# Threshold attention and a squared-ReLU layer on one core: where the second weight chunk's load stands among the loads of the second attention period

## Chip, cores and metric

The kernel runs on one core of a Trainium2 chip. Its time is device microseconds (us) of that core. A number given for a kernel is the median of three runs; a profile is one further execution, with its own time.

## The reference, cut to what matters

Attention over 8 batches of 8 heads, 576 positions, head size 64. A weight survives only where its score is within `tau` of the row's maximum. The result, reshaped to 4608 tokens of 512, goes through two matrices with a squared ReLU between them.

```python
scores = q @ k.T / 8
scores = where(scores >= max(scores) - tau, scores, -1e9)
attn = exp(scores - max(scores)); attn /= sum(attn) + 1e-9
x = (attn @ v).transpose(0, 2, 1, 3).reshape(4608, 512)
h = maximum(x @ w_in, 0)                 # w_in 512 x 2048
out = h * h @ w_out                      # w_out 2048 x 512
```

The two weight matrices arrive in eight-byte floating point: NumPy makes them so by the factor they are scaled with. q, k and v are four-byte.

## The kernel before

**Three stages.** First attention (to about 512 us of the profile), then the hidden layer, then the output layer. The two layers multiply 128x128 blocks by a scheme that saves products and pays with sums on VectorE (DVE) and GpSimd (POOL). The weights for them are brought in and made four bytes wide during attention, in 32 chunks.

**Attention in periods.** The heads are taken in 32 pairs (two heads side by side in 128 partitions). A pair's queries are cut into units of 128 rows; `period(p)` (L619) works on two units, A = 2p and B = 2p+1, and runs over p = -2 ... 74. Within one period:

- `SA`, `SB`: the scores of A and B on TensorE (PE), L434.
- `topA0` ... `topB1`: DVE copies the scores out of PSUM and takes each row's extreme, L452. `powA0` ...: the exponential on ScalarE (ACT), L462. `maskA0` ...: DVE masks and sums, L467. `least` and `over` are tiny POOL steps (L459, L474), `inv` is DVE's reciprocal (L477), which needs `over`.
- `U`, `V`, `W`: PE turns the masked weights of the periods before (L380, and L515 for the reciprocals, which needs `inv`); `eU`, `eV`, `eW` are ACT's copies of these out of PSUM (L523).
- `PV`: the product with the values (L532); `x` copies it out (L657 on ACT in a period that converts), `xm` scales it on POOL (L669) and queues it to be written out (L578).
- `T`: PE turns the queries or the keys of a pair that will be needed later (L398); `eT` has ACT copy them out (L403, L411) **and then asks for loads of a later pair** through `ask_ahead` (queries `load_q`, L294; keys `load_k`, L308, L315, L316).
- `fetch`: issues the load of one weight chunk, 512 KB, on SyncE's (SP's) DMA queue (L191). `c1` ... `c6` make a chunk four bytes wide: c1 on ACT (L205), c3 on POOL (L219), c2 on POOL (L212), and one period later c4 and c5 on DVE (L227, L235) and c6 on POOL (L245).

**What sets the order.** Every engine carries out its own instructions in the order in which the program issues them, and that order is a list of step names written by hand: `PLAIN`, `CONVERTING`, and in `BEGIN_WITH` (L602) lists of their own for periods 0 and 1. Nearly all loads and stores of this stage stand in one queue, SP's, in program order.

**Chunks and periods.** `fetch(begun(p + 2))` in period p loads the chunk whose c1 stands in period p + 2: chunk 0 is fetched in period 0, chunk 1 in period 1, chunk 2 in period 2. Period 2 is the first with the list `CONVERTING`, in which `fetch` is the first step and c1 stands ahead of `powA0`. A chunk lands in one of four buffers of its own, so the fetches of chunks 0 to 3 wait for no earlier user.

**Turns and loads.** `TURNS` puts the queries of pair 1 in period 0, its keys in period 1, the queries of pair 2 in period 2, its keys in period 3, the queries of pair 3 in period 4, its keys in period 5. `ask_ahead` of period 0 asks for the queries of pairs 2 and 3 (four loads), that of period 1 for the keys of pairs 2 and 3 (seven loads each), that of period 2 for the queries of pair 4.

So SP's queue holds, from period 0 on: chunk 0, four query loads, fourteen key loads, chunk 1, chunk 2, two query loads, and so on.

Of the kernel before, what the change touches and what calls it, by code (L numbers as in the profile page):

```python
# [48 lines left out]
def kernel(  # L49
# [539 lines left out]
    def begun(n):  # L589
# [15 lines left out]
            maskA0 maskA1 maskB0 maskB1  # L605
        """.split(),
        1: """
            SA SB T eT fetch over topA0 topA1 leastA inv V topB0 topB1 leastB powA0 powA1 eV W
            powB0 eW maskA0 maskA1 powB1 maskB0 maskB1
        """.split(),  # L610
    }
# [627 lines left out]
```

## Time and profile before

| what | value |
|---|---|
| median of three runs | 1308.43 us (1307.17 to 1308.57) |
| the profiled execution: time | 1308.95 us |
| the profiled execution: span, first to last instruction | 1307.2 us |
| mean granted TensorE clock | 0.995 |
| busy: PE, DVE, POOL, ACT | 98%, 77%, 70%, 65% of the span |
| chunk loads of `w_in` (512 KB each) | 16, median 4.5 us from issue to landing |
| loads of keys (64 KB) | 126, median 3.1 us from issue to landing |

The times of the profile are microseconds from the span's start. A row of the timeline gives start, duration, engine, line, operation, output and input, and in brackets how long the engine stood idle before and what released it. "SPq" rows are SP's issues of DMAs, not the transfers. Periods begin, by the first score product of `SA`, near 22 (SB of period 2 stands at 22.1), 27.9 (period 3), 38.0 (period 4) and 46.1 us (period 5).

### The profile page before, as it was taken

How to read it: one execution, taken by the hardware profiler on the slowest of the kernel's cores; microseconds unless marked ns; L12 is line 12 of the kernel's file. 1: busy time of each engine (PE TensorE's matmuls, PEld its weight loads, DVE VectorE, ACT ScalarE, POOL GpSimd, SP SyncE). 2: the span in 40 equal slices, each digit the busy share in tenths (PEclk: the TensorE clock that was granted, in tenths of full speed). 3: DMA queues.
4: the chain of work that ended last, by engine and by line, in shares of the span. 5: the costliest groups of instructions: out<-in, count | busy, mean ns of one | idle time of the engine just before them, and what ended most of it. 6: DMA issues, size and time to landing. Idle time of an engine off the chain costs nothing.

```text
span 1307.2 us, 47836 instructions
## 1 busy us (share of the span) xinstructions
PE 1283.6 (98%) x19463; PEld 1158.4 (89%) x19463; DVE 1010.1 (77%) x2431; ACT 846.1 (65%) x1498; POOL 915.6 (70%) x1023
## 2 busy tenths in 40 slices
PE   8899999999999999999999999999999999999998
PEld 5677777777777778999999999999999999999998
DVE  6899999999999996877787778777646654665463
ACT  5999999988999985657665766675523432433240
POOL 2778788765555320978897889768777777777775
PEclk8999999999999999999999999999999999999999
DMA  5665666544433313466656665579645224522511
GB/s 126 165 158 144 169 180 191 147 103 101 94 78 79 81 39 80 140 192 218 195 169 194 215 196 166 176 262 396 226 157 162 72 95 159 161 65 99 161 33 33
DMA packets 247035, 192.12 MB, mean 147 GB/s; under 512 B 97184, under 2 KB 195488, under 8 KB 246816
## 3 DMA queue, kind: packets, MB, share of 16 engines
q1 hardware_dynamic: 245504, 188.66, 48.0%
q8 instruction: 153, 2.51, 0.8%
q14 instruction: 66, 0.54, 0.1%
q10 hardware_dynamic: 1312, 0.41, 0.1%
HBM read 116.65 MB, written 72.35 MB: 145 GB/s over the span
## 4 chain that ended last, share of the span: by engine, by line
PE 88%; ACT 4%; DVE 3%; DMA 2%; issue 1%; SPq 1%; POOL 0%; ACTq 0%; POOLq 0%; DVEq 0%
PE ph L840 29%; PE po L975 29%; PE sc L532 10%; PE sc L434 10%; PE pt L380 5%; DVE arena L452 2%; PE sc L515 2%; PE sc L398 2%; ACT arena L462 2%; ACT arena L523 1%; PE sc L380 1%; DMA wall<-w 1%; DMA arena<-in_q_dram 1%; DMA g<-arena 0%; DMA arena<-in_moe_w_in_dram 0%
## 5 line engine op out<-in xcount | busy, mean ns | idle before, releaser
L125 POOL TENSOR_TENSOR arena<-arena 128x512 f32<-128x512 f32 (+1 forms) x314 | 377.8, 1222 | 134.9 <-DVE arena L125 116.6
L975 PE MATMUL po<-wall,arena 128*128 128x128 f32 x3528 | 395.0, 276 | 1.8 <-ACT arena L752 1.4
L975 PEld LDWEIGHTS po<-wall,arena 128*128 128x128 f32 x3528 | 394.3, 192 | 2.4 <-ACT arena L752 1.8
L840 PE MATMUL ph<-arena,wall 128*128 128x128 f32 x3528 | 394.2, 275 | 0.7 <-DVE arena L659 0.7
L840 PEld LDWEIGHTS ph<-arena,wall 128*128 128x128 f32 x3528 | 394.0, 192 | 0.8 <-issue 0.8
L125 DVE TENSOR_TENSOR arena<-ph,arena 128x512 f32<-128x512 f32 x378 | 256.4, 689 | 86.2 <-PE ph L840 66.3
L122 POOL TENSOR_TENSOR arena<-arena 128x128 f32<-128x128 f32 (+2 forms) x314 | 254.8, 812 | 48.8 <-DMA arena<-w 32.6
L467 DVE SCALAR_TENSOR_TENSOR arena<-arena 128x576 f32<-128x576 f32 x288 | 236.5, 857 | 2.2 <-ACT arena L462 1.3
L125 DVE TENSOR_TENSOR arena<-po,arena 128x128 f32<-128x128 f32 x378 | 108.3, 290 | 167.9 <-PE po L975 163.7
L452 DVE TENSOR_SCALAR_CACHE_REDUCE arena<-sc 128x576 f32<-128x576 f32 x288 | 205.2, 748 | 12.3 <-ACT arena L523 4.1
L462 ACT ACTIVATE arena<-arena 128x576 f32<-128x576 f32 x288 | 208.8, 774 | 8.1 <-DVE arena L452 5.1
L786 ACT COPY c<-arena 128x512 f32<-128x512 f32 (+1 forms) x303 | 173.5, 580 | 50.5 <-DVE arena L122 41.3
L532 PEld LDWEIGHTS sc<-arena 64*64 64x64 f32 x5760 | 159.2, 133 | 36.3 <-DVE arena L452 20.3
L532 PE MATMUL sc<-arena 64*64 64x128 f32 (+1 forms) x5760 | 180.4, 263 | 2.7 <-DVE arena L452 1.1
L434 PE MATMUL sc<-arena 64*64 64x64 f32 (+1 forms) x2304 | 177.5, 417 | 4.8 <-ACT arena L403 2.3
L122 DVE TENSOR_TENSOR arena<-arena,c 128x512 f32<-128x512 f32 (+1 forms) x267 | 174.9, 663 | 6.0 <-ACT c L786 4.0
L523 ACT COPY arena<-pt 128x1024 f32<-128x1024 f32 x144 | 146.2, 1016 | 29.7 <-PE pt L380 28.4
L752 ACT COPY arena<-po 128x128 f32<-128x128 f32 x63 | 16.6, 263 | 186.5 <-PE po L975 183.7
L380 PEld LDWEIGHTS pt<-ident,arena 64*128 64x128 f32 x2304 | 84.0, 140 | 40.9 <-ACT arena L523 28.3
L752 ACT COPY arena<-ph 128x512 f32<-128x512 f32 x63 | 36.6, 581 | 124.2 <-PE ph L840 123.7
L434 PEld LDWEIGHTS sc<-arena 64*64 64x64 f32 x2304 | 74.4, 134 | 42.7 <-issue 15.5
L380 PE MATMUL pt<-ident,arena 64*128 64x64 f32 x2304 | 102.8, 230 | 3.2 <-ACT arena L523 2.2
(51 smaller groups left out, 917.6 us busy)
## 6 DMA issues: line engine op xcount, KB each, us to landing
g<-arena SPq DMA_DIRECT2D x144, 256.0 KB, 2.5
arena<-g SPq DMA_DIRECT2D x144, 256.0 KB, 4.5
w<-arena SPq DMA_DIRECT2D x60, 256.0 KB, 2.4
wall<-w SPq DMA_DIRECT2D x49, 256.0 KB, 5.2
arena<-w SPq DMA_DIRECT2D x44, 256.0 KB, 3.0
arena<-in_v_dram SPq DMA_DIRECT2D x32, 288.0 KB, 3.9
out_dram<-arena SPq DMA_DIRECT2D x70, 128.0 KB, 2.2
arena<-in_q_dram SPq DMA_DIRECT2D x64, 128.0 KB, 3.8
```

What stands on the lines that cost most here:

```text
L122: e.tensor_tensor(out=out, in0=x, in1=y, op=ALU.subtract)
L125: e.tensor_tensor(out=out, in0=x, in1=y, op=ALU.add)
L380: made = nc.tensor.transpose(pt[:, r, ts(slot, HALF)], of[rows, :], ident[rows, rows])
L434: made = nc.tensor.matmul(sc[at, ds(to, count)], lhs, kT[rows, ds(at_k, count)], start=True, stop=True)
L452: made = nc.vector.tensor_scalar(out=s[:, j, :], in0=sc[:, ds(at, S)], scalar1=1.0, scalar2=None, op0=ALU.mult, op1=ALU.min, accum_out=nmx ...
L462: nc.scalar.activation(out=w[:, :, j, :], in_=of(j), func=AF.Exp, bias=nmx[:, j : j + 1], scale=-1.0)
L467: nc.vector.scalar_tensor_tensor(out=w[:, :, j, :], in0=of(j), scalar=thr[:, j : j + 1], in1=w[:, :, j, :], op0=ALU.is_le, op1=ALU.mult, a ...
L523: touch("weights", nc.scalar.copy(joined(to), whole(pt, 0, count)), at, 2 * BANK, m)
L532: made = nc.tensor.matmul(sc[ds(u * D, D), ds(5 * j * BANK + row, count)], loaded_v[i][rows, (c - (u != j)) % CH, :], wT[m][rows, ds(weigh ...
L786: nc.scalar.copy(c, y)
L840: nc.tensor.matmul(to[:, j, :], W_IN[m, k][:, ts(j, P)], of[k][:, m - 1, :], start=(not more and j == 0), stop=True, skip_group_check=True,)
L975: nc.tensor.matmul(to, g[:, j, :], w[:, j, :], start=(not more and j == 0), stop=(j == 3), skip_group_check=True)
```

## The change

In the list of period 1, `fetch` moves from behind `T eT` to the front. Nothing is added or removed: the same instructions are issued, and on SP's queue the load of chunk 1 (one DMA, L191) moves ahead of the fourteen loads of the keys of pairs 2 and 3 that `eT` of this period asks for.

```diff
         1: """
-            SA SB T eT fetch over topA0 topA1 leastA inv V topB0 topB1 leastB powA0 powA1 eV W
+            fetch SA SB T eT over topA0 topA1 leastA inv V topB0 topB1 leastB powA0 powA1 eV W
             powB0 eW maskA0 maskA1 powB1 maskB0 maskB1
         """.split(),
```

## The prediction

> **What bounds the kernel now.** I read from the whole to the place of the change. The page gives PE 98% of the span and 88% of the chain that ended last, but that is a mean over three stages. A table by stretches of 25 us (columns: span of the stretch, then busy us and instructions of PE, PE's weight loads, DVE, ACT, POOL, then clock, DMA share, GB/s) shows what is full in the attention stage:
>
> ```profile
> 43.00:68.00 25.00, 24.91 (x656) 19.48 (x657) 25.00 (x68) 24.07 (x47) 19.77 (x26) 1.00 0.55 143
> ...
> 218.00:243.00 25.00, 24.61 (x581) 18.11 (x582) 25.00 (x70) 24.33 (x43) 20.66 (x27) 1.00 0.70 194
> ```
>
> DVE is busy for 25.00 of 25.00 us in these two, and for at least 24.94 in each of the eight stretches from 43 to 243 us. From 43 us on, whatever brings DVE to a given instruction earlier moves all that follows; before 43 us DVE has holes. Next, who waits for the chunk that the change moves. The waits of ACT between 28 and 43 us:
>
> ```profile
> ACT arena L205 <- DMA arena<-in_moe_w_in_dram: 3.3, 1, 3.3
> ```
>
> One wait of 3.3 us, for a weight chunk, at L205, which is c1. The chain that ended last passes through it (start, duration, what):
>
> ```profile
> 28.96 0.60 SPq L316
> 29.56 0.04 issue
> 29.60 4.73 DMA arena<-in_moe_w_in_dram
> 34.33 0.02 issue
> 34.35 0.02 ACT arena L205
> ```
>
> So chunk 1 is issued at 29.60, right behind the last of the key loads, lands at 34.33, and ACT stands from 31.02 to 34.35. What this does to DVE (timeline of DVE, rows with idle time, and the one before):
>
> ```profile
> 33.03 0.42 DVE L227 TENSOR_SCALAR arena<-arena 128x512 int32<-128x512 int32 x1
> 36.32 0.18 DVE L477 RECIPROCAL arena<-arena 128x4 f32<-128x4 f32 x1 [2.86 <-POOL arena L474]
> ...
> 41.14 0.76 DVE L452 TENSOR_SCALAR_CACHE_REDUCE arena<-sc 128x576 f32<-128x576 f32 x1 [0.57 <-PE sc L398]
> ...
> 42.99 0.76 DVE L452 TENSOR_SCALAR_CACHE_REDUCE arena<-sc 128x576 f32<-128x576 f32 x1 [0.41 <-issue]
> ```
>
> The first hole is the chunk's: c1 on ACT, then c3 and `over` on POOL (L474 at 36.05), then `inv`. The other two are its echo: PE waited 2.22 us for `inv` and 1.00 us for ACT's `x`, and then ran period 4 at half clock:
>
> ```profile
> 35.78:39.19 3.41, 1.64 (x36) 1.24 (x38) 2.87 (x8) 3.41 (x9) 3.17 (x4) 1.00 0.93 269
> 39.19:42.60 3.41, 3.41 (x48) 1.91 (x38) 2.76 (x7) 2.82 (x5) 2.67 (x4) 0.50 0.18 39
> ```
>
> PE was busy 1.64 of 3.41 us, and in the next 3.41 us the granted clock was 0.50; L434's eight products (SB) took 1.84 us there against 1.09 in period 3. [...]
>
> **What the change removes and adds.** No instruction is added. On SP one issue moves past the fourteen key loads that `eT` of period 1 asks for. SP's timeline from there:
>
> ```profile
> 14.27 2.03 SPq L294 DMA_DIRECT2D arena<-in_q_dram  x4
> 16.34 4.42 SPq L308 DMA_DIRECT2D arena<-in_k_dram  x2
> ...
> 24.30 0.60 SPq L316 DMA_DIRECT2D arena<-in_q_dram  x1
> ```
>
> *The fetch itself.* It would be issued at 16.34. SP holds the first key load there for 3.76 us (to 20.1), an issue that elsewhere takes 0.6; the profile names no semaphore for it, and 4 query loads, chunk 0 and values are under way. I take it that the fetch is held likewise: issue over by 20.1 at the latest. Landings in the trace follow the order of issue: chunk 0 20.29, the four query loads 20.84, 21.45, 22.16, 22.64. Chunks issued back to back land 1.56 us apart (34.33, 35.89), so chunk 1 lands near 22.64 + 1.56 = 24.2; with the 4.73 us of its own row from 20.1, 24.8. ACT asks for it at 31.02: **6 us of slack**, the wait of 3.33 us is gone.
>
> *The keys of pair 2*, seven loads, are what the fetch now stands ahead of. Before, they are issued to 24.91 and the last lands at 27.07; T of period 3 turns them at 29.80, so there are 2.7 us of slack. The fetch costs SP one issue, 0.43 to 0.5 us, and its 1.56 us of transfer lie in the queue while SP needs 0.6 us for each key load anyway, so most of that is hidden. I take the last landing at 27.6 (one issue later); the upper end is 28.7 (0.5 + 1.56 - 0.4). Both are before 29.80. The keys of pair 3 come half a us later and are wanted in period 5, at 48.
>
> *The rest of SP's queue.* As many issues stand ahead of chunk 2 as before, so it is still issued near 30, but without chunk 1 ahead of it lands near 34.5 and not at 35.89.
>
> **Period 3 again, without the wait.** ACT: c1 at 31.02, the exponentials 31.6 to 33.7, `eT` to 34.5, `x` to 34.9 (PV is over at 34.06). POOL's `over` came 1.97 us after c1's start (36.32 - 34.35), so at 33.0; DVE ends L227 at 33.45, so `inv` follows with no hole: 2.86 us won. Behind it DVE has its five instructions of period 3 (36.32 to 40.57, 4.25 us) and ends at 37.7. PE: W's last part at 34.3 instead of 36.55, SA of period 4 at 34.9 instead of 38.01; PE has no gap left worth a clock spell, so at full clock T is over at 37.4 (1.4 + 0.7 + 0.5) and SB at 38.5. DVE's first copy of period 4 needs T: 37.4 against 37.7, the 0.57 is gone. Its third needs SB: 38.5 against 39.1, the 0.41 is gone. **What is late next**: chunk 2 at 34.5 against ACT's c1 near 38.1, and POOL, which works on to 39.2 and then does c3 with `over` at 40.4 against DVE's `inv` at 40.9. Both hold, the last by 0.5 us only.
>
> Sum: 2.86 + 0.57 + 0.41 = **3.84 us**, all of them holes of the engine that has none for the next 200 us. After that, order and dependences are the same and start earlier; the only transfer on the chain up to 500 us is a store of 2.22 us at 263.68, itself started by POOL's work. In the layers PE is full and starts earlier. Against the profiled execution: 1308.95 - 3.84 = 1305.1. That execution is 0.5 us above the median of the runs, so the median becomes 1308.43 - 3.84 = **1304.6 us**.
>
> Where I chose: if the clock spell is only luck and comes all the same, 2.86 us are won (1305.6). If a full 3.33 us of ACT plus the difference of the two periods' lengths (38.01 to 46.12 is 8.11, the next 6.76: 1.35) were won, it would be 4.7 us (1303.7), but DVE has not that many holes. Half-clock spells around 18.7 to 25.5 us may shift from run to run as well; by the same 1.35 us I bound that to either side.
>
> **Rivals.**
>
> 1. *The keys take the chunk's place.* SP stays blocked at the first key load until chunk 1 is through, at 24.2: then the other six are issued as before (24.91 - 20.11 = 4.8 us) to 29.0, and the last lands 2.16 us later, at 31.2. T of period 3 is 1.4 us late, DVE's first copy with it: 3.84 - 1.4 = 2.4 won, 1306.0. For it: the 3.76 us hold happened in just this place. Against it: two chunks back to back were issued in 1.68 us and two query loads behind them in 0.93, with no such hold.
> 2. *Slower.* The same place, but held twice: the fetch leaves SP only at 20.5, the first key load waits until it has landed (20.5 + 4.73 = 25.2), seven issues at their pace end at 30.6 and land at 32.8, and the 0.9 us by which one L315 was late before (1.49 against 0.6) comes on top: 33.7. T is 3.9 us late, which eats the gain; PE's gap brings the half clock back (0.98 of DVE holes). 3.84 - 3.9 - 0.98 = 1.0 lost: 1309.4. It decides from a landing at 32.7 on, which is 5.6 us later than before.
> 3. *The chunk shares the engines with the queries in front of it.* Queries of pair 2 land at 21.45 and PE waits for them (0.44 us, then DVE 1.68). If chunk 1's packets take turns with theirs, T of period 2 is up to 1.56 us later: 2.3 won, 1306.1. Against: the landings were in order of issue. [...]
> 4. *Given back later*: the chain is elastic somewhere behind 243 us, where DVE has holes again (24.2 of 25), and nothing is left: 1308.4.
>
> **Chances.** The forecast 0.71 (its own range 1303.4 to 1305.8), rivals 1 and 3 together 0.14, rival 4 0.06, rival 2 (slower) 0.09. The range takes in the forecast's and rivals 1 and 3 with the spread of the runs: 1303.0 to 1307.4. A measurement here tells about 0.2% (2.6 us) from no change: faster by more than that takes the forecast and a share of rivals 1 and 3, 0.74; within it 0.17; slower 0.09.
>
> **What would show it.** Right: ACT's L205 of period 3 starts near 31.0 with no wait for the chunk; `inv` directly behind L227 at 33.5; SA of period 4 near 34.9; clock 1.00 around 36 to 40; DVE at its first copy of period 5 near 44.9 instead of 48.70, and full from 30 us on. Rival 1 or 2: L398 of period 3 waits for a key load. Rival 3: L398 of period 2 starts later than 21.49. The forecast is wrong if chunk 1 lands after 31, or if DVE shows a new hole between 33 and 43 us, first of all before `inv` of period 4.

## The result, and the profile after

The changed kernel takes 1304.73 us (median of eight runs, 1302.06 to 1306.6), the kernel before 1308.53 us in the same series (median of eight, 1307.17 to 1310.59): 3.8 us less, a ratio of 0.9967 [0.9957, 0.9978] (in brackets, here and below, the 95% interval). Its profiled execution took 1305.30 us with a span of 1303.5; that of before 1308.95 with 1307.2. PE, DVE, ACT and POOL run the same instructions in the same order; only SP's queue differs.

**ACT.** The view of waits of ACT between 28 and 43 us is empty. Before, it held the wait of 3.3 us for the chunk and one of 0.6 us for PE at L523 (40.77), which the prediction left out. The timeline of ACT at period 3 shows c1 right behind the copy before it:

```profile
29.55 1.01 ACT L523 COPY arena<-pt 128x1024 f32<-128x1024 f32 x1
30.46 0.68 ACT L205 ACTIVATE arena<-arena 128x512 f32<-128x512 f32 x1
```

**DVE.** Its timeline of the changed kernel has no row with idle time between 30 and 45 us. The first copy of period 3, and the three places where there were holes:

```profile
30.13 0.75 DVE L452 TENSOR_SCALAR_CACHE_REDUCE arena<-sc 128x576 f32<-128x576 f32 x1
...
32.85 0.42 DVE L227 TENSOR_SCALAR arena<-arena 128x512 int32<-128x512 int32 x1
33.18 0.16 DVE L477 RECIPROCAL arena<-arena 128x4 f32<-128x4 f32 x1
...
37.20 0.75 DVE L452 TENSOR_SCALAR_CACHE_REDUCE arena<-sc 128x576 f32<-128x576 f32 x1
...
38.56 0.74 DVE L452 TENSOR_SCALAR_CACHE_REDUCE arena<-sc 128x576 f32<-128x576 f32 x1
...
44.27 0.74 DVE L452 TENSOR_SCALAR_CACHE_REDUCE arena<-sc 128x576 f32<-128x576 f32 x1
```

The last row is the first copy of period 5. The same two copies, of periods 3 and 5, in the kernel before:

```profile
30.32 0.75 DVE L452 TENSOR_SCALAR_CACHE_REDUCE arena<-sc 128x576 f32<-128x576 f32 x1
...
48.70 0.75 DVE L452 TENSOR_SCALAR_CACHE_REDUCE arena<-sc 128x576 f32<-128x576 f32 x1
```

From here on a **stretch** means the time from DVE's first copy (`topA0`) of period 3 to that of period 5: 18.38 us before, 14.14 after, so 4.24 us came out of these two periods.

**PE.** The table by windows, for the same 6.8 us as in the prediction (busy and instructions of PE, weight loads, DVE, ACT, POOL; clock; DMA share; GB/s):

```profile
35.78:39.19 3.41, 3.27 (x69) 2.09 (x68) 3.41 (x10) 3.38 (x6) 2.50 (x3) 1.00 0.63 177
39.19:42.60 3.41, 3.41 (x106) 2.87 (x98) 3.41 (x11) 3.30 (x8) 3.17 (x5) 1.00 0.30 58
```

The clock is 1.00 in both, and in the second of them PE gets 106 products done where it did 48.

**SP.** Its timeline shows the price of the move (start, duration of the whole group, line, what, how many):

```profile
17.37 2.55 SPq L191 DMA_DIRECT2D arena<-in_moe_w_in_dram  x1
19.96 1.26 SPq L308 DMA_DIRECT2D arena<-in_k_dram  x2
...
23.87 1.22 SPq L316 DMA_DIRECT2D arena<-in_q_dram  x1
```

The fetch is held for 2.55 us in the place where the first key load was held for 3.76; the key loads behind it go out at 0.6 us each, but for the last (L316), which takes 1.22. By the trace's landing records chunk 1 lands at 23.98, the last key load of pair 2 at 27.21, chunk 2 at 34.23.

**The chain that ended last** no longer holds a load between 16 and 44 us. Where it stood on the chunk's landing at 34.33 before and passed on through ACT, it now runs through PE's products and DVE's copies of period 4 (start, duration, what):

```profile
36.28 0.25 PE sc L398 x7
36.53 0.74 PE sc L434 x5
37.28 0.48 DVE arena L452
```

### The profile page after: what moved, and what is told of

The parts are those of the page before. It is cut to its first block, busy times and chain, and to the rows that moved or that the text cites. A ratio compares the mean times of both kernels' runs of the same rounds, so it can differ in the third digit from the quotient of the medians.

```text
span 1303.5 us, 47836 instructions
## 1 busy us (share of the span) xinstructions
PE 1283.4 (98%) x19463; PEld 1158.6 (89%) x19463; DVE 1010.0 (77%) x2431; ACT 846.2 (65%) x1498; POOL 914.6 (70%) x1023
## 4 chain that ended last, share of the span: by engine, by line
PE 87%; ACT 4%; DMA 3%; DVE 3%; issue 1%; POOL 1%; SPq 0%; ACTq 0%; POOLq 0%; DVEq 0%
PE ph L840 28%; PE po L975 28%; PE sc L532 11%; PE sc L434 10%; PE pt L380 5%; DVE arena L452 2%; DMA wall<-w 2%; PE sc L515 2%; PE sc L398 2%; ACT arena L462 1%; ACT arena L523 1%; PE sc L380 1%; DMA arena<-g 0%; DVE arena L125 0%; DMA g<-arena 0%
## 5 line engine op out<-in xcount | busy, mean ns | idle before, releaser
L523 ACT COPY arena<-pt 128x1024 f32<-128x1024 f32 x144 | 146.4, 1017 | 30.3 <-PE pt L380 29.1
```

Source lines behind the costliest of these rows:

```text
L523: touch("weights", nc.scalar.copy(joined(to), whole(pt, 0, count)), at, 2 * BANK, m)
```

## The experiments

A ratio is against the kernel before, run beside it (its medians were 1308.46 to 1309.2 us). Single runs of one kernel lie up to 4 us from its median, so the medians of kernels that differ by 1 us are not told apart. The stretch on DVE, taken from one profile each, is finer: behind the first copy of period 5 the rest of the span is 1258.4 to 1259.9 us in every kernel.

| kernel | ACT's wait for chunk 1 | stretch | half clock between 35 and 45 us | median, ratio |
|---|---|---|---|---|
| before | 3.33 | 18.38 | 39.19, for 3.41 us | 1308.53 |
| before, again (b1) | 4.54 | 20.38 | 36.47, for 6.83 | |
| before, again (b2) | 4.21 | 19.92 | 37.14, for 6.83 | |
| changed | none | 14.14 | none | 1304.73, 0.9967 |
| changed, again (a1) | none | 14.15 | none | 1303.98, 0.9964 |
| e1 | none | 14.13 | none | 1305.55, 0.9986 |
| e2 | 0.4 | 14.12 | none | 1305.98, 0.9982 |
| e3 | none | 14.13 | none | 1305.98, 0.9977 |
| e4 | none | 14.13 | none | 1304.3, 0.9974 |
| e5 | none (c1 late) | 15.44 | none | 1306.64, 0.9987 |
| e6 | 0.57 (c1 late) | 15.44 | none | 1305.37, 0.998 |
| g1 | none | 14.15 | none | 1304.22, 0.9968 |
| w1 | 2.02 | 22.07 | 37.86, for 6.83 | 1315.97, 1.0057 |
| w2 | 5.59 | 20.21 | 39.04, for 3.41 | 1308.5, 1.0003 |

The theory: ACT's wait for chunk 1 opened the hole ahead of `inv`, the other two holes followed from it, and any place of the fetch that lands the chunk before ACT asks for it gives the same gain. The rivals: the place itself matters, because the key loads, the query loads or SP pay for it; or the time came from something else that the new order brings, and not from the wait.

### e1: behind the keys of pair 2

```diff
-            asked[which] += 1
+            asked[which] += 1; fetch(1 if (which, asked[which]) == (1, 3) else None)
...
-            SA SB T eT fetch over topA0 topA1 leastA inv V topB0 topB1 leastB powA0 powA1 eV W
+            SA SB T eT over topA0 topA1 leastA inv V topB0 topB1 leastB powA0 powA1 eV W
```

> Chunk 1's fetch behind the seven key loads of pair 2 and ahead of those of pair 3. The theory (the whole difference is ACT's wait for chunk 1 ahead of the exponentials, and the DVE holes it makes): issued near 25, it lands near 29.7, still before ACT asks near 30.5 to 31; no wait, so the time of the changed kernel: 3.8 us below the kernel before, about 1304.7. Rival A (what counts is how early the chunk stands in the queue, since the order of the loads around it changes too): about half of the gain, 1306.6. Rival B (the clock spells decide, the load does not): the difference to the kernel before goes with the clock, not with the place.

Measured: 1305.55 us (twelve runs, 1304.54 to 1308.89), 0.9986 [0.9975, 0.9997]. The chunk was issued at 22.54 and landed at 27.70, with no wait of ACT and a stretch of 14.13. The keys of pair 2 had nothing new in front of them, and the stretch is that of the changed kernel, where the chunk stands ahead of them: there it took nothing from these keys that PE or DVE felt in the stretch. The median is another matter: by the ratio e1 wins 0.1% and the changed kernel 0.3%, and the two intervals barely overlap. Seven of e1's runs had a mean granted clock of 0.997 and took 1305.29 to 1306.71 us; the changed kernel's three runs with that clock took 1305.30 to 1306.60. But e1 has two runs at 0.996 (1308.70 and 1308.89) and none at 0.999 or 1.000, where the changed kernel has three (1302.06 to 1304.94). So the medians differ with the granted clock of the runs; whether the place of the load has a part in that is not shown.

### e2: among the keys of pair 3

```diff
-            queue = nc.scalar if i == 0 and j == 0 else nc.sync
+            fetch(1 if (i, j) == (3, 1) else None); queue = nc.scalar if i == 0 and j == 0 else nc.sync
...
-            SA SB T eT fetch over topA0 topA1 leastA inv V topB0 topB1 leastB powA0 powA1 eV W
+            SA SB T eT over topA0 topA1 leastA inv V topB0 topB1 leastB powA0 powA1 eV W
```

> Chunk 1's fetch amid the keys of pair 3, four loads ahead of its old place. The theory: issued near 27.2, landed near 31.9, ACT waits about 1.2 us; POOL's sum has 0.8 us to spare before DVE's reciprocal wants it, so a DVE hole of 0.3 to 0.6 us, no PE gap and no half clock in period 4: 3.2 to 3.5 us below before, about 1305.2. Rival A (one us of ACT's wait costs one us and more, as 3.33 us cost 4.25 us of DVE time between the first copies of periods 3 and 5): 1.2 us of wait cost 1.5 us, so 2.3 us below before, 1306.2.

Measured: 1305.98 us (twelve, 1303.63 to 1308.6), 0.9982 [0.9971, 0.9992]. The chunk landed at 29.75, earlier than expected, since SP's hold at the first key load was 1.78 us here and not 3.76. The view of ACT's waits:

```profile
ACT arena L205 <- DMA arena<-in_moe_w_in_dram: 0.4, 1, 0.4
```

That wait cost nothing: DVE had no hole and the stretch is 14.12. `inv` comes behind four copies and L227 on DVE, and a c1 that is 0.4 us late is still in time for it. So the price of a wait on ACT isn't its length, but what of it shows as a hole on DVE.

### e3: ahead of the queries of pair 2

```diff
         0: """
-            SA SB fetch topA0 T topA1 leastA topB0 topB1 leastB powA0 powA1 eT powB0 powB1
+            SA SB fetch fetch1 topA0 T topA1 leastA topB0 topB1 leastB powA0 powA1 eT powB0 powB1
...
+            "fetch1": lambda: fetch(1),
```

with the step taken out of the list of period 1.

> Chunk 1's fetch in period 0, right behind chunk 0 and ahead of the four query loads. The theory (landings in order of issue, 1.56 us for a chunk): the queries of pair 2 land near 22.9 instead of 21.3, and T of period 2, which stood at 22.3 in the changed kernel and waited for nothing, starts 0.6 to 1.5 us later; so 0.6 to 1.5 us slower than the changed kernel, about 1305.8, still 2.3 to 3.2 us below before. Rival (the transfers share the engines, so the place ahead of the queries costs them nothing more than the place behind): the time of the changed kernel, 1304.7.

Measured: 1305.98 us (twelve, 1303.77 to 1308.6), 0.9977 [0.9966, 0.9988], stretch 14.13. Here something pays in the profile, one period earlier. PE and DVE in period 2 of e3:

```profile
22.79 0.47 PE L398 MATMUL sc<-ident,arena 64*128 64x64 f32 x8 [1.29 <-DMA arena<-in_q_dram]
```

```profile
23.26 0.76 DVE L452 TENSOR_SCALAR_CACHE_REDUCE arena<-sc 128x576 f32<-128x576 f32 x1 [2.64 <-PE sc L398]
```

and DVE's same row in the changed kernel:

```profile
22.97 0.76 DVE L452 TENSOR_SCALAR_CACHE_REDUCE arena<-sc 128x576 f32<-128x576 f32 x1 [1.45 <-PE sc L398]
```

PE waits 1.29 us for queries that it did not wait for, and DVE's hole is 1.19 us larger. The transfers landed in the order of issue (queries of pair 2 at 22.10 and 22.65, behind the chunk at 21.69), which is what the prediction's third rival supposed of the other place and did not get there. But this hole is 0 to 1.7 us in the other thirteen profiles, so its size is not settled by one of e3. Nor did the loss reach period 3, which begins at 29.89 here and at 30.13 in the changed kernel's profile, whose early spell of half clock was longer (6.83 us against 3.41). The median can't show a loss of this size.

### e4: three chunks ahead of all the keys

```diff
-            SA SB T eT fetch over topA0 topA1 leastA inv V topB0 topB1 leastB powA0 powA1 eV W
+            fetch fetch2 fetch3 SA SB T eT over topA0 topA1 leastA inv V topB0 topB1 leastB powA0 powA1 eV W
...
+            "fetch": lambda: p in (2, 3) or fetch(begun(p + 2)), "fetch2": lambda: fetch(2), "fetch3": lambda: fetch(3),
```

> Chunks 1, 2 and 3 all at the front of period 1, ahead of the keys (periods 2 and 3 fetch none). This prices the rivals of the prediction in which the keys of pair 2 come late. The theory: two more chunks put 3.1 us of transfer and 1 us of issue ahead of the keys, which landed at 27.34 in the changed kernel with T of period 3 at 29.34: they land at 29 to 31, T is 0 to 1.7 us late, so the time lies between that of the changed kernel and 1.7 us above it (1304.7 to 1306.4). Rival 2 of the prediction (SP holds the next issue until a chunk has landed, chunk by chunk): the keys land at 33 or later and the time is that of the kernel before or above, 1308.5 to 1310.

Measured: 1304.3 us (ten, 1303.47 to 1306.59), 0.9974 [0.9963, 0.9985], stretch 14.13. SP's timeline, and PE's at the turns of pair 2's keys in period 3:

```profile
16.62 2.48 SPq L191 DMA_DIRECT2D arena<-in_moe_w_in_dram  x3
19.14 1.26 SPq L308 DMA_DIRECT2D arena<-in_k_dram  x2
```

```profile
28.44 0.48 PE L398 MATMUL sc<-ident,arena 64*128 64x64 f32 x10
```

The turns show no wait. Three chunks took SP no longer than one does in the changed kernel (2.48 against 2.55 us): its hold is no price for each chunk. Six of the seven key loads landed at 25.53 to 27.88 (the record of the seventh, issued last, can't be told from that of a later load), so at most 0.56 us were left before the turns at 28.44; in the changed kernel all seven have landed at 27.21 (not 27.34, as the expectation has it), 2.1 us before the turns at 29.34. One chunk has ample room ahead of these keys, and two more use up most of it.

### e5 and e6: the old order of loads, with c1 later

If the wait is the cause, it can be removed without moving any load: c1 and c3 of period 3 go behind `x`, and ACT's exponentials no longer stand behind the chunk.

```diff
+    LATE_C1 = [s for x in CONVERTING if x not in ('c1', 'c3') for s in ([x, 'c1', 'c3'] if x == 'x' else [x])]
...
-        for name in BEGIN_WITH.get(p) or (CONVERTING if converts(p) else PLAIN):
+        for name in LATE_C1 if p == 3 else BEGIN_WITH.get(p) or (CONVERTING if converts(p) else PLAIN):
```

> The load order of the kernel before, undisturbed; in period 3 alone c1 and c3 of chunk 1 stand behind x instead of ahead of the exponentials, so ACT does not stand before them. The theory: chunk 1 lands near 34.3, when ACT has done the exponentials, eT and x (near 34.3), so no wait in front of the reciprocal, no DVE hole at 33.5, no PE gap, clock 1.00 in period 4: the changed kernel's time, 1304.7, with the load as late as before. Rival A (the gain comes from the loads' new order): the time of the kernel before, 1308.5.

Measured: 1306.64 us (twelve, 1304.95 to 1308.16), 0.9987 [0.9977, 0.9997]. The chunk landed at 32.08, after the time at which ACT used to ask for it. No wait for it, no half clock, no hole ahead of `inv`, none of the two behind it, but a new one on DVE:

```profile
36.41 1.34 DVE L467 SCALAR_TENSOR_TENSOR arena<-arena 128x576 f32<-128x576 f32 x1 [1.07 <-POOL arena L459]
```

A mask waits for `leastB`, which now stood behind c3 on POOL. e6 moves c3 on, behind `leastB`:

```diff
+    LATE_C1 = [s for x in CONVERTING if x not in ('c1', 'c3') for s in {'x': ['x', 'c1'], 'c2': ['c3', 'c2']}.get(x, [x])]
```

> As e5 (old load order; c1 of chunk 1 behind x), with c3 behind leastB as well. In e5 the stretch of DVE from period 3 to 5 was 15.44 us and not 14.1, since POOL's c3 stood ahead of leastB, which DVE's second mask pair needs. The theory (ACT's wait ahead of the exponentials and POOL's in front of the small steps make the whole difference): 14.1 to 14.3 us now, although chunk 1 is loaded as late as before; total 1304.7 to 1305. Rival A (the order of the loads): 15.4 as in e5, or more.

Measured: 1305.37 us (eleven, 1303.65 to 1306.93), 0.998 [0.9971, 0.9988]. The stretch is 15.44 again and not the 14.1 to 14.3 expected. DVE's rows with idle time:

```profile
36.29 0.83 DVE L467 SCALAR_TENSOR_TENSOR arena<-arena 128x576 f32<-128x576 f32 x1 [1.02 <-ACT arena L462]
40.66 0.18 DVE L477 RECIPROCAL arena<-arena 128x4 f32<-128x4 f32 x1 [0.48 <-POOL arena L474]
```

POOL's hole is gone and ACT's took its place: the chunk landed at 33.96, ACT still stood 0.57 us in front of the late c1, and the exponential behind it came late. What both show: with the loads as late as before, taking the wait out of the way of the exponentials wins most of the stretch (18.4 to 20.4 down to 15.4), and the rest, 1.3 us, is the price of doing c1 late, through POOL in e5 and through ACT in e6. No version had the old order of loads and neither of these holes, so that the order itself costs nothing is shown to within these 1.3 us. By the medians the share is less sharp: e6 wins 0.1 to 0.3%, e5 0.0 to 0.2%, the changed kernel 0.2 to 0.4%.

### b1, b2, a1: both kernels once more

> The kernel before, profiled once more, since the span of the other profiles moves by an us or two before period 3. From DVE's first copy of period 3 to its first copy of period 5 the kernel before took 18.38 us, and every kernel whose chunk 1 landed in time 14.1. The theory: ACT waits again for chunk 1, and this stretch is again above 14.1; how far depends on how long SP holds its first key load (3.76 us in the first profile, 1.6 to 1.8 in later ones), so that the wait may lie between 1.2 and 3.3 us and the stretch between 14.6 and 18.4. Rival B (a stroke of the clock in that one profile): 14.1 with no wait.

> The same once more, with the same two expectations: between 14.6 and 18.4 us by the theory, 14.1 by rival B. If the wait is short and PE has no gap in period 4, the half clock of 39 to 43 us should be missing, and then the stretch is longer than 14.1 by the wait less some 0.8 us of POOL's slack.

> The changed kernel once more, beside the others of this call: 3.8 us below the kernel before (1304.7), no wait of ACT for chunk 1, the stretch from period 3 to 5 on DVE 14.1 us, half clock only ahead of period 3. What may vary is the start: DVE's first copy of period 3 between 29 and 31 us, and the earlier half-clock spell 3.4 or 6.8 us long.

Measured: the kernel before took 1310.97 and 1310.65 us in these two executions (one each), the changed kernel 1303.98 (six, 1303.31 to 1305.78), 0.9964 [0.995, 0.9978]. DVE's holes in the first of them:

```profile
35.92 0.18 DVE L477 RECIPROCAL arena<-arena 128x4 f32<-128x4 f32 x1 [3.85 <-POOL arena L474]
41.68 0.76 DVE L452 TENSOR_SCALAR_CACHE_REDUCE arena<-sc 128x576 f32<-128x576 f32 x1 [1.51 <-PE sc L398]
43.62 0.76 DVE L452 TENSOR_SCALAR_CACHE_REDUCE arena<-sc 128x576 f32<-128x576 f32 x1 [0.49 <-ACT arena L462]
```

The three holes are the same ones with other sizes: 5.85 us in all here, 5.38 in b2 (3.45, 1.51, 0.42), 3.84 in the profile that the prediction read. Landing and wait differ with them: 33.93 and 4.54 us in b1, 34.72 and 4.21 in b2. The profiled executions of before lie 0.5, 2.5 and 2.2 us above its median, so the median's loss may be nearer to 3.84 than to these. Both stretches lie above what was expected (14.6 to 18.4 us), and not for the reason given there: SP held its first key load for less time than in the first profile (3.29 and 2.65 us against 3.76), and the wait was longer all the same.

### w1, w2 and g1: is the half clock an echo of PE's gap?

w1 gives PE twenty turns of the identity, whose results nobody uses, in the old order, where it stood waiting:

```diff
+    warm = lambda m, n: [nc.tensor.transpose(sc[:, ds(2 * BANK + 3 * P, P)], ident[:, :], ident[:, :]) for _ in range(n if m == 2 else 0)]
...
-            rs = smalls.pop(m)
+            rs = smalls.pop(m); warm(m, 14)
...
-                scores(A, False)
+                warm(p - 2, 6); scores(A, False)
```

> The kernel before with 20 turns of the identity added on PE, 14 in front of W's last part of period 3 and 6 in front of period 4's first scores, where PE stood idle for ACT's wait; their results go to unused columns. Chunk 1 is as late as before. The theory (the half clock after the wait is an echo of PE's gap and costs 1.4 to 2.4 us of the 18.4 to 20.4 us from DVE's first copy of period 3 to that of period 5): no half-clock spell between 35 and 45 us, the reciprocal's hole as large as before (2.9 to 3.9 us), the stretch 14.1 plus that hole plus at most 0.5, so 17 to 18.3 us, and the time 1.4 to 2.4 us below the kernel before, about 1306.5. Rival B (spells come as they like): a spell there as before, the stretch and the time unchanged.

Measured: 1315.97 us (five, 1313.48 to 1316.92), 1.0057 [1.0043, 1.0071]. It failed as a test. PE's rows:

```profile
36.95 2.41 PE L486 MATMUL sc<-ident 128*128 128x128 f32 x14 [2.39 <-ACT arena L657]
...
40.76 1.54 PE L486 MATMUL sc<-ident 128*128 128x128 f32 x6 [0.76 <-ACT arena L523]
```

The turns waited for ACT's copies of other results themselves, so the gap stayed and the work was added to it. w2 declares them apart from those banks and puts all twenty around the last part of W.

> As w1, mended: there the added turns of the identity waited for ACT's copies out of other banks, so that PE had its gap all the same. Now they are declared apart from the other banks, and all 20 stand around W's last part of period 3 (14 ahead, 6 behind). Chunk 1 is as late as in the kernel before. The theory (the half clock is an echo of PE's gap): no half-clock spell between 35 and 45 us; the stretch on DVE from period 3 to 5 is 14.1 plus the reciprocal's hole (1.4 to 3.9 us, by how late the chunk is) plus at most 0.5, and the time 1.4 to 2.4 us below the kernel before: about 1306.5 to 1307. Rival B (spells come as they like): a spell there as in all three profiles of the kernel before, the stretch 18 us or more, the time that of the kernel before, 1308.5 to 1309.

Measured: 1308.5 us (twelve, 1306.59 to 1311.71), 1.0003 [0.9992, 1.0014]. In the profile the chunk kept ACT waiting for 5.59 us, the longest of all, and PE was through with the turns before `inv` came:

```profile
32.92 1.75 PE L486 MATMUL sc<-ident 128*128 128x128 f32 x14
37.01 0.46 PE L515 MATMUL sc<-ident,arena 64*64 64x64 f32 x16 [2.35 <-DVE arena L477]
```

A gap of 2.35 us remained, and so did the half clock. Inconclusive. What stands is a coincidence in all fourteen profiles: a gap on PE of 2.2 to 3.3 us behind the late chunk, and half clock after it, in the five with c1 waiting ahead of the exponentials for over 2 us; neither in the other nine.

g1 puts six such turns into T of period 1 of the changed kernel, ahead of the half clock that the start of the kernel shows.

```diff
+                rows = ds(r * HALF, HALF); [nc.tensor.transpose(spot[:, ds(3 * P, P)], ident[:, :], ident[:, :]) for _ in range(6 if (i, which, t, r) == (1, 1, FULL, 0) else 0)]
```

> The changed kernel with 6 turns of the identity on PE in T of period 1, ahead of the last two turns of the keys of pair 1, where PE waited 0.7 us for a load in the profile; results go to unused columns. It asks whether the earlier half-clock spell (3.4 or 6.8 us from about 17 to 25 us) is worth removing. If 0.8 us more of PE's work keeps it away: DVE's first copy of period 3 at 28.5 to 29 instead of 29 to 31, and the time 1 to 1.5 us below the changed kernel, 1303.4. If not: the changed kernel's time, or up to 0.8 us more where the load is not late and the turns only delay T.

Measured: 1304.22 us (five, 1303.31 to 1306.03), 0.9968 [0.9955, 0.9981]. Its profile has no spell of half clock in attention, and DVE's first copy of period 3 stands at 28.51 (28.99 in a1, 30.13 in the first profile of the changed kernel). The mean granted clock was 1.000 in three of its five runs, against two of the changed kernel's eight and none of a1's six. The median is no better than a1's, so no version here beats the changed kernel by what can be measured.

## Why the prediction was right, point by point

**The wait and the first hole.** As forecast: c1 has no wait, `inv` stands directly behind L227 (33.18; forecast 33.5), and SA of period 4 at 34.29 (34.9). e2, e5 and e6 show that it was the wait, and that only its part beyond DVE's own work counts.

**The sum.** 3.84 us forecast, 4.24 in the profiled pair. The holes were named rightly and each is a little larger than its bracket says: back to back, a row on DVE begins 0.07 to 0.09 us before the one ahead of it ends (33.18 against 32.85 + 0.42), so by starts the three holes are 2.96, 0.65 and 0.49, and 0.15 came from the masks between. The spell of half clock, of which the prediction left open whether it was luck, came in every profile in which ACT waited for over 2 us, from 36.5 to 39.2 us on. No run shows how far the earlier half clock moves by itself, for which the prediction put 1.35 us: it lay at 18.71 to 25.54 us in the profile before and at 16.69 to 23.52 in the changed kernel's, and two profiles of one kernel have DVE's first copy of period 3 1.37 us apart (30.32 in the first of before, 28.95 in b1).

**The fetch and the keys.** Chunk 1 landed at 23.98 (forecast 24.2), the last key load of pair 2 at 27.21 (27.6), chunk 2 at 34.23 (34.5). SP was held at the fetch for 2.55 us and behind it only at the last of these keys (1.22 us instead of 0.6), with 2.1 us of room left before the turns, so the first two rivals found nothing; e1 and e4 give the same stretch with no chunk moved in front of those keys and with three.

**The queries.** The sign that the prediction named for rival 3 did show: L398 of period 2 starts later than 21.49.

```profile
22.30 0.64 PE L398 MATMUL sc<-ident,arena 64*128 64x64 f32 x8
```

It was a poor sign, since a start moves with everything ahead of it (chunk 0's fetch stands at 14.74 here and at 13.72 before). The row has no wait for a load, where the one before waited 0.44 us, so rival 3 got nothing in the changed kernel. In e3, where the chunk stands ahead of the queries, PE did wait for them.

**What is late next.** `over` of period 4 ends at 40.01 on POOL and `inv` starts at 40.25: 0.24 us of slack instead of 0.5, enough.

**Given back.** DVE is 4.4 us ahead at period 5 (4.24 from the stretch, 0.2 from an earlier start of period 3), and the span is 3.7 us shorter. Where the difference went is seen by taking DVE's instructions one by one: the lead is 4.4 us up to 386 us of the changed kernel, and two steps take from it. Two of DVE's copies, before:

```profile
399.84 0.76 DVE L452 TENSOR_SCALAR_CACHE_REDUCE arena<-sc 128x576 f32<-128x576 f32 x1
...
459.20 0.76 DVE L452 TENSOR_SCALAR_CACHE_REDUCE arena<-sc 128x576 f32<-128x576 f32 x1 [0.35 <-ACT arena L523]
```

and the same two in the changed kernel:

```profile
395.81 0.76 DVE L452 TENSOR_SCALAR_CACHE_REDUCE arena<-sc 128x576 f32<-128x576 f32 x1 [0.45 <-ACT arena L523]
...
455.53 0.76 DVE L452 TENSOR_SCALAR_CACHE_REDUCE arena<-sc 128x576 f32<-128x576 f32 x1 [0.67 <-ACT arena L523]
```

DVE waits there for ACT's copies, once anew and once for longer, so the lead falls to 4.03 us and then to 3.67, where it stays to the end: a small piece of rival 4. Why ACT's copies come later there was not found. Terms 0.4 too small and 0.7 given back nearly cancel, with the 0.2 of the start, so the median's agreement to 0.1 us (1304.6 and 1304.73) is partly luck; the mechanism and its place are not.

**What the prediction took as fixed.** It read one execution and took ACT's wait of 3.33 us for that of the kernel. In the six other profiles of the old order of loads the chunk landed between 32.1 and 34.8, and where c1 stood in its old place ACT waited 2.0 to 5.6 us. That the forecast met the median rests in part on a profile that was near the median.

**Left open.** No run settles whether the half clock needs PE's gap (w1 and w2 did not take the gap away); the last section shows how busy PE was ahead of it. Why SP's hold varies is open too.

## What to carry to other kernels

Price a wait by the holes that it opens on the engine that is full in that stage, not by its own length: 3.33 us on ACT was 4.24 us of DVE here, and 0.4 us was nothing. Here the load needed only to land before a wait for it could show on DVE: by the stretch (14.12 to 14.15 us), no place was better than another between landings at 24.0 and 29.7. Ahead of the queries (e3) PE waited 1.29 us for what was wanted sooner. Where a wait ends with a transfer, look at several executions before taking its length as a property of the kernel.

## What was not expected of the hardware

**SP's hold moves about.** The first issue behind the four query loads took 1.5 to 3.8 us in fourteen profiles (most other issues 0.4 to 0.6), whether it was a key load or a chunk, and some later issue mostly 1.2 to 2.2 us. In the old order chunk 1 stood behind all of this, so its landing moved with it: b1 reached DVE's first copy of period 3 1.37 us earlier than the first profile of before (28.95 against 30.32), but the chunk came only 0.40 us earlier (33.93 against 34.33). What holds SP, no profile names.

**Half clock while PE had work.** The spells in attention lasted 3.41 or 6.83 us. PE was not idle all the time ahead of them, which the prediction's rows show already: it was busy for 1.64 of the 3.41 us ahead of the spell. Ahead of the earlier one, at 18.71 in the same profile, it was 1.70 of 3.41 us. In w2 it was 1.84, and the spell came all the same:

```profile
35.63:39.04 3.41, 1.84 (x28) 1.41 (x32) 2.26 (x6) 3.41 (x9) 3.17 (x5) 1.00 0.99 281
39.04:42.45 3.41, 3.41 (x52) 2.73 (x48) 2.20 (x6) 2.23 (x4) 2.96 (x3) 0.50 0.29 57
```

In the kernel before, the 3.42 us just ahead of those with 1.64 us of work held a little more, and full clock followed:

```profile
32.36:35.78 3.42, 1.97 (x68) 1.66 (x60) 1.09 (x5) 1.43 (x3) 0.68 (x2) 1.00 1.02 311
```

At the other end, PE in b1 was busy for 0.31 us from 33.06 to 36.47, with a clock of 0.50 in the 3.41 us behind. In the changed kernel the emptiest of four such rows from 28.95 to 42.60 held 3.27 us, and the clock was 1.00 in all of them. This is the profile's busy time, with modelled ends of the products. What decides the clock is not shown.
